# One accumulator per PSUM bank, attention output scaled into SBUF, layer-1 weight bounds by TensorE products, and a new planned order

## The chip, the core and the metric

The kernel runs on one core of a Trainium2 chip. The core has TensorE (matrix products, which stand in the profile as PE, with its weight loads apart as PEld), VectorE (DVE), ScalarE (ACT), GpSimd (POOL) and the SyncE queue (SP), which issues all DMAs here. The metric is the device time of one execution in microseconds (us), lower is better. Every instruction stands in its engine's queue in program order; an instruction that waits holds up all that stand behind it on that engine.

## The reference

Attention over 4 batches, 8 heads, 576 positions and head size 64, with a bias from a small network, then two pairs of dense layers on the 2304 x 512 result:

```python
scores = scale * q @ k.T
x = log1p(|i - j|) / log1p(max(i, 1))            # i, j: positions
scores = scores + relu(x * w1 + b1) @ w2          # one bias per head
attn = exp(scores - max(scores)); attn = attn / (sum(attn) + 1e-9)
x = (attn @ v) as [2304, 512]
x = (s * relu(x @ w_in)**2 + b) @ w_out           # layer 1: 512 -> 2048 -> 512
h = x @ w_in2; return (h - tanh(h)) @ w_out2      # layer 2: 512 -> 2048 -> 512
```

The four big weight matrices arrive as 64-bit floats, all else as 32-bit floats.

## The kernel before

**Arithmetic.** Each operand of a product is split into two 16-bit floats, a high and a low part, under a power-of-two scale, and each product is taken as three (high x high, high x low, low x high). The scales need bounds: the largest norm of the weights of layer 1 is found on the chip before they are split.

**Stages.** (1) Start, to about 150 us: VectorE turns the 64-bit weights of layer 1 into 32-bit (three instructions a piece, L1248, L1251, L1254), they are bounded (squares on ScalarE, L1306 and L1347; column sums by TensorE against ones, L1313), scaled and split (L619 high, L622 low; the high part may go to ScalarE or VectorE). Meanwhile q, k, v are prepared, the bias network is worked out (L726 and L729 hidden units, L760 product) and the first attention units run. (2) Attention and layer 1 overlapped, to about 575 us: 160 units (one head and one chunk of 128 rows each, or two heads of 64 rows) in 36 groups of four, 9 blocks of 256 rows for layer 1. (3) The rest of layer 1 from about 575 to 707 us, while the weights of layer 2 are converted and split. (4) Layer 2 to the end: Strassen-like products of 24 matrix instructions each (L2019 in, L2149 out).

**A unit**: scores into PSUM (L1040, two units at a time), bias added and maximum taken (VectorE, L1072), exponential (ScalarE, L1086), high and low part (L1096 or L1098, and L1103 on GpSimd or VectorE), a DMA transpose, then 14 matrix instructions into the accumulator `xp` (L1131, L1137). After the four units of a group: the row sums are inverted, `xp` is multiplied by them in place (VectorE, L1184), copied to a 16-bit high part (L1192 or L1194), the low part is the difference (L1198), and ScalarE squares `xp` for the norm (L1201). All four read the accumulator in PSUM.

**Layer 1, a block**: 16 products of 12 matrix instructions into `ph` (L1554), two at a time, relu (L1567), square (L1572), split (L1578/L1580, L1584); then 4 accumulators `po`, each of 4 products of 12 (L1626, 48 instructions in all), each moved out by L1645 (ScalarE) or L1640 (VectorE) in two or three pieces.

**PSUM** has 8 banks: 4 for scores (ring `s`), 2 for `ph` and small sums (ring `h`), one for `po`, one for `xp`. The tile `po` is [128, 2, 256] and `xp` too: two halves of one bank are used in turn, and the planner's rings `o` and `x` have two places each.

**Order.** A planner (`Schedule`) writes the whole program. Every task has its engines with a cost (`COST`, `XFER`), a due time with a correction from a table (`SHIFT`), a choice of engine (`ENGINE`), and rings that it takes places in; the planner walks through time with these figures, takes on each engine the task that is due first among those ready, and writes instructions in that sequence. When the program is built, waits are put in from what each instruction reads and writes; those of PSUM go by the whole bank, so an instruction on one half waits for one on the other half that stands ahead of it.

## Time and profile before

| | |
|---|---|
| runs, median (lowest to highest) | 1066.86 us (1065.9 to 1069.4) |
| the profiled execution | 1063.98 us, of it the span from first to last instruction 1062.2 us |
| busy in the span | PE 957.4 (90%), DVE 869.7 (82%), ACT 687.5 (65%), POOL 249.5 (23%) |
| mean granted clock of TensorE | 0.955 of full speed |

Busy shares are means over stages with different limits: in the start VectorE and ScalarE are full and TensorE is not, in the second half TensorE is. So the rows below are taken by stage. A busy PE need not be at its peak, since matrix instructions overlap.

### The profile page before, as it was taken

Reading aid. Unit: us, or ns where it says so; the run is one execution under the profiler, and the core shown is the slowest. Engines: PE = TensorE matmul, PEld = TensorE weight load, DVE = VectorE, ACT = ScalarE, POOL = GpSimd, SP = SyncE. Lnnn points to the kernel's source line nnn. Section 1 sums busy time; section 2 is a strip of 40 time slices with the busy share of each in tenths; the row PEclk is TensorE's granted clock in tenths of the full one; section 3 lists DMA queues with packets and bytes.
Section 4 is the critical chain, followed back from the end, with each engine's and each line's share of the span. In section 5 each row is a group of like instructions: output and inputs, shape, how many; then the busy total and the mean of one; then the engine's idle time right before and its main releaser. Section 6 shows DMA issues by size and latency. Waiting matters only on the chain.

```text
span 1062.2 us, 32293 instructions
## 1 busy us (share of the span) xinstructions
PE 957.4 (90%) x13370; PEld 821.9 (77%) x13370; DVE 869.7 (82%) x1902; ACT 687.5 (65%) x1357; POOL 249.5 (23%) x305
## 2 busy tenths in 40 slices
PE   5646679998999899999999998978999999999998
PEld 3213346787777788778877887868999999999998
DVE  6999997754658687878774879889999999898876
ACT  5998898668667586665734686866635546564433
POOL 6234455445456323355420000000000000000000
PEclk9867679999999999999999999999999999999999
DMA  9979998799999889989995905310111100100000
GB/s 344 395 233 247 308 211 171 165 241 234 221 186 232 167 188 190 186 157 198 166 172 94 399 13 162 117 40 2 32 32 42 42 22 25 39 22 23 23 22 22
DMA packets 261444, 153.66 MB, mean 145 GB/s; under 512 B 197680, under 2 KB 229552, under 8 KB 261296
## 3 DMA queue, kind: packets, MB, share of 16 engines
q1 hardware_dynamic: 261296, 151.59, 58.6%
q8 instruction: 104, 1.70, 0.7%
q14 instruction: 44, 0.36, 0.1%
HBM read 84.03 MB, written 20.33 MB: 98 GB/s over the span
## 4 chain that ended last, share of the span: by engine, by line
PE 70%; DVE 10%; ACT 9%; DMA 6%; issue 4%; SPq 1%; POOL 0%; DVEq 0%; ACTq 0%; POOLq 0%
PE po L1626 16%; PE ph L1554 14%; PE acc L2149 13%; PE pa L2019 8%; PE pb L2019 6%; PE sp L1040 4%; PE xp L1131 3%; PE po L2149 2%; DMA et<-hl 2%; PE pb L760 2%; ACT e L1086 2%; DVE sp L1072 1%; PE xp L1137 1%; ACT x L1645 1%; DMA w1big<-in_win 1%
## 5 line engine op out<-in xcount | busy, mean ns | idle before, releaser
L1626 PE MATMUL po<-hr,w1big 128*128 128x256 f16 x1728 | 203.3, 274 | 14.6 <-ACT x L1645 10.6
L1103 POOL TENSOR_TENSOR hl<-e,hl 128x512 f16<-128x512 f32 (+1 forms) x185 | 158.8, 871 | 191.5 <-ACT hl L1098 76.9
L1626 PEld LDWEIGHTS <-w1big 128*128 128x128 f16 x1728 | 166.4, 98 | 38.8 <-issue 19.4
L1554 PEld LDWEIGHTS <-w1big 128*128 128x128 f16 x1728 | 166.4, 99 | 31.0 <-issue 11.2
L2019 PEld LDWEIGHTS <-w2big 128*128 128x128 f16 x3024 | 175.1, 99 | 8.6 <-issue 8.6
L2149 PEld LDWEIGHTS <-w1big 128*128 128x128 f16 x3024 | 172.7, 98 | 0.0
L1086 ACT ACTIVATE e<-sp,mx 128x576 f32<-128x576 f32 x144 | 105.7, 736 | 57.8 <-POOL mx L1080 26.7
L1072 DVE CUSTOM_DVE_ANT_0 sp<-sp,bi 128x576 f32<-128x576 f32 x144 | 107.0, 775 | 34.9 <-PE sp L1040 30.1
L1554 PE MATMUL ph<-xt_own,w1big 128*128 128x256 f16 x960 | 115.1, 276 | 3.8 <-ACT r L1567 3.3
L1040 PE MATMUL sp<-ks,qs 64*128 64x288 f16 (+1 forms) x960 | 81.4, 299 | 19.5 <-ACT e L1086 19.2
L1554 PE MATMUL ph<-w1big 128*128 128x256 f16 x768 | 90.8, 276 | 0.3 <-DVE na L1513 0.3
L1131 PEld LDWEIGHTS <-et 128*128 128x128 f16 (+1 forms) x1440 | 55.8, 104 | 38.8 <-issue 21.4
L1040 PEld LDWEIGHTS <-qs 64*128 64x128 f16 (+1 forms) x960 | 46.0, 100 | 46.7 <-issue 33.6
L1131 PE MATMUL xp<-vp,et 128*128 128x64 f16 (+1 forms) x1440 | 65.7, 199 | 15.9 <-DMA et<-hl 6.3
L2149 PE MATMUL acc<-hr,w1big 128*128 128x128 f16 x1296 | 79.7, 219 | 0.0
L2149 PE MATMUL acc<-w2big,w1big 128*128 128x128 f16 x1296 | 79.2, 219 | 0.0
L1103 DVE TENSOR_TENSOR hl<-e,hl 128x512 f16<-128x512 f32 (+1 forms) x103 | 52.8, 526 | 12.3 <-ACT hl L1098 7.0
L2019 PE MATMUL pa<-w1big,w2big 128*128 128x128 f16 x960 | 61.2, 221 | 1.2 <-ACT w1big L2038 0.9
L1096 DVE CAST hl<-e 128x576 f16<-128x576 f32 x71 | 38.5, 543 | 24.5 <-ACT e L1086 17.4
L1645 ACT ACTIVATE x<-po,bcol,esc 128x128 f32<-128x128 f32 (+1 forms) x69 | 26.7, 443 | 48.6 <-PE po L1626 46.3
L1567 ACT ACTIVATE r<-ph 128x512 f32<-128x512 f32 x72 | 42.5, 592 | 19.3 <-PE ph L1554 18.1
L1098 ACT ACTIVATE hl<-e 128x576 f16<-128x576 f32 x73 | 48.9, 679 | 7.3 <-DMA et<-hl 6.9
(225 smaller groups left out, 1767.0 us busy)
## 6 DMA issues: line engine op xcount, KB each, us to landing
bi<-btd SPq DMA_DIRECT2D x64, 288.0 KB, 3.9
w1big<-in_wout SPq DMA_DIRECT2D x12, 1024.0 KB, 5.9
btd<-et SPq DMA_DIRECT2D x36, 295.5 KB, 4.5
w1big<-in_win SPq DMA_DIRECT2D x8, 1024.0 KB, 10.7
w2big<-in_win SPq DMA_DIRECT2D x8, 1024.0 KB, 13.0
x2d<-x SPq DMA_DIRECT2D x36, 128.0 KB, 2.0
w1big<-x2d SPq DMA_DIRECT2D x36, 128.0 KB, 2.3
outT<-xt_own SPq DMA_DIRECT2D x18, 256.0 KB, 2.2
```

The source lines that it names most:

```text
L1040: nc.tensor.matmul(out=out, lhsT=qs.tile[64 * h:64 * h + 64, sq, p * r:p * r + r], rhs=ks.tile[64 * h:64 * h + 64, sk, half * HS:(half + 1 ...
L1072: nc.vector.tensor_tensor_reduce(out=st, in0=st, in1=bi.tile.rearrange("p (a b) -> p a b", a=2), scale=-1.0 / KAP, scalar=3.0e38, op0=ALU. ...
L1086: nc.scalar.activation(out=put(e, row_tile("e")).rearrange("p (a b) -> p a b", a=2), in_=sp.tile[:, :, 0:HS], func=AF.Exp, scale=-1.0, bia ...
L1096: nc.vector.tensor_copy(out=h[:, 0:S], in_=e.tile)
L1098: nc.scalar.activation(out=h[:, 0:S], in_=e.tile, func=AF.Copy)
L1103: eng_of(eng).tensor_tensor(out=hl.tile[:, o:o + m], in0=e.tile[:, c:c + m], in1=hl.tile[:, c:c + m], op=ALU.subtract)
L1131: nc.tensor.matmul(out=xp[r0:r0 + r, o:o + 64], lhsT=et.tile[:, n, r0:r0 + r], rhs=vp.tile[:, 0, n % 5, 64 * h:64 * h + 64], start=n == 0, ...
L1554: nc.tensor.matmul(out=ph.tile[:, fi, :], lhsT=win_ap(1, sw, m, f), rhs=xa(sx, m), start=m == 0 and j == 0, stop=m == KM - 1 and j == 2,)
L1567: nc.scalar.activation(out=r.tile, in_=ph.tile, func=AF.Relu)
L1626: nc.tensor.matmul(out=po.tile[:, :NB1], lhsT=wout_ap(1, sw, f, c), rhs=rhl[f // 8][:, f % 8, sr, :], start=f == 0 and j == 0, stop=f == K ...
L2019: nc.tensor.matmul(out=bank.tile[:, f * HT:(f + 1) * HT], lhsT=w[:, sw, m, f * 128:(f + 1) * 128], rhs=xs[:, sx, m], start=p in (1, 2, 5) ...
L2149: nc.tensor.matmul(out=bank.tile[:, o + c * HT:o + (c + 1) * HT], lhsT=w[:, sw, f, c * 128:(c + 1) * 128], rhs=g[:, sx, f], start=new and ...
```

## The change

`po` and `xp` become one accumulator each: `po_tile` gives always the first half, `xp` shrinks to [128, 256], and the rings `o` and `x` have one place. The scaled attention output goes to a new SBUF tile `xf` (two buffers), and the high part, the low part and the squares read `xf`; the low part may now run on GpSimd. The bound of the layer-1 weights comes from TensorE: each 128-column block of a converted weight piece, read as its upper 16 bits, is multiplied by itself (16 matrix instructions for each of 8 weight parts), and VectorE takes maxima; the 16 squares on ScalarE and the 16 products against ones go. For the in-weights the maximum over partitions is taken with one more product against a unit matrix. The high part of a layer-1 weight may run on GpSimd. The tables and hop times of the planner are new, and with them the whole order. All lines below L455 shift, so `po` products are L1645, `ph` products L1573, `xp` products L1132 and L1138 in the new program.

```diff
@@ -28,13 +28,13 @@
-AHEAD = 8.71
+AHEAD = 6.97
 COST = {
...
@@ -42,16 +42,16 @@
-    0.98, "f.lo@dve": 0.98, "f.hi@act": 1.09, "f.hi@pool": 1.09, "u.hi@pool": 1.12, "u.ex@dve": 0.96,
...
@@ -59,152 +59,153 @@
-    "s1.lambda": "dve", "bias0.out": "act", "f0.hi": "act", "f1.hi": "act", "u7.hi": "act", "bias3.out": "act",
+    "s1.lambda": "dve", "f1.hi": "act", "bias3.out": "act", "bias4.lambda": "dve", "k1.hi": "act", "f2.hi":
...
-    ".begin": 3275.8, ".fn": -302.4, ".lambda": 973.3, "I0.add": -26.1, "I0.fn": 420.3, "I0.lambda": 110.4,
+    ".begin": 158.6, ".eye": 204.2, ".fn": -49.3, ".lambda": 60.6, "I0.add": 1197.4, "I0.fn": -551.5,
...
@@ -264,7 +265,7 @@
-    HOP = dict(pe=0.33, act=-0.03, dve=0.16, pool=0.4, turn=0.0)
+    HOP = dict(pe=0.57, act=-0.03, dve=0.16, pool=0.37, turn=0.0)
@@ -454,11 +455,9 @@
 
 
     po_all = ps_o.tile([128, 2, 256], F32, name="po")
-    po_n = [0]
 
     def po_tile():
-        po_n[0] += 1
-        return po_all[:, po_n[0] % 2, :]
+        return po_all[:, 0, :]
 
     ctx.enter_context(tc.manual_schedule())
 
@@ -569,12 +568,7 @@
-    xp_all = ps_x.tile([128, 2, 256], F32, name="xp")
-    xp_c = [0]
-
-    def xp_n():
-        xp_c[0] += 1
-        return xp_c[0] % 2
+    xp_all = ps_x.tile([128, 256], F32, name="xp")
@@ -586,8 +580,8 @@
-        ("bi", 4), ("e", 2), ("hl", 3), ("et", 4), ("stg", 4), ("qst", 1), ("qs", 2), ("ks", 8), ("vp", 8), ("s", 2), ("x", 2),
-        ("h", 2), ("o", 2), ("r", 2), ("xt", 4), ("x2", 2), ("xh", 2), ("sum", 4),
+        ("bi", 4), ("e", 2), ("hl", 3), ("et", 4), ("stg", 4), ("qst", 1), ("qs", 2), ("ks", 8), ("vp", 8), ("s", 2), ("x", 1),
+        ("h", 2), ("o", 1), ("r", 2), ("xt", 4), ("x2", 2), ("xh", 2), ("xf", 2), ("sum", 4),
@@ -615,6 +609,8 @@
     def copy_scale(out, in_, c, eng):
         if eng == DVE:
             nc.vector.tensor_scalar(out=out, in0=in_, scalar1=c, scalar2=None, op0=ALU.mult)
+        elif eng == POOL:
+            nc.gpsimd.tensor_scalar(out=out, in0=in_, scalar1=c, scalar2=None, op0=ALU.mult)
         else:
             nc.scalar.activation(out=out, in_=in_, func=AF.Copy, scale=c)
 
@@ -679,11 +675,16 @@
-        nc.vector.memset(ones16, 1.0)
+
+    def eye(_):
+        nc.gpsimd.affine_select(
+            out=eye32, in_=ones32, pattern=[[-1, 128]], compare_op=ALU.is_equal, fill=0.0, base=0, channel_multiplier=1,
+        )
+    t_eye = sc.add({POOL: 1.7}, eye, [t_one], prio=-1e5)
@@ -1122,7 +1123,7 @@
-                put(xp_i, xp_all[:, xp_n(), :])
+                put(xp_i, xp_all)
@@ -1179,28 +1180,32 @@
             nc.vector.reciprocal(out=sum_of[n].tile, in_=sum_of[n].tile)
         te = sc.add({DVE: 0.17}, recip, [te], d - 2, [], [sum_of[n]])
 
+        xf = inst("xf")
+
         def scale(_):
             x = xp_of[n].tile.rearrange("p (h d) -> p h d", d=64)
+            put(xf, x_p.tile([128, 256], F32, tag="xf", name="xf", bufs=2))
             nc.vector.tensor_tensor(
-                out=x, in0=x, in1=sum_of[n].tile.unsqueeze(2).to_broadcast([128, NP, 64]), op=ALU.mult,
+                out=xf.tile.rearrange("p (h d) -> p h d", d=64), in0=x,
+                in1=sum_of[n].tile.unsqueeze(2).to_broadcast([128, NP, 64]), op=ALU.mult,
             )
-        t_xs[n] = sc.add({DVE: 0.41}, scale, [t_pv[u] for u in us] + [te], d - 500, [], [sum_of[n], xp_of[n]])
+        t_xs[n] = sc.add({DVE: 0.41}, scale, [t_pv[u] for u in us] + [te], d - 500, [xf], [sum_of[n], xp_of[n]], share=0.0)
 
         def hi(eng):
             put(xh, x_p.tile([128, 512], F16, tag="xh", name="xh", bufs=2))
             if eng == DVE:
-                nc.vector.tensor_copy(out=xh.tile[:, 0:256], in_=xp_of[n].tile)
+                nc.vector.tensor_copy(out=xh.tile[:, 0:256], in_=xf.tile)
             else:
-                nc.scalar.activation(out=xh.tile[:, 0:256], in_=xp_of[n].tile, func=AF.Copy)
-        th = sc.add({DVE: 0.36, ACT: 0.45}, hi, [t_xs[n]], d - 100, [xh], [xp_of[n]], share=0.0)
-
-        def lo(_):
-            nc.vector.tensor_tensor(out=xh.tile[:, 256:512], in0=xp_of[n].tile, in1=xh.tile[:, 0:256], op=ALU.subtract)
-        th = sc.add({DVE: 0.42}, lo, [th], d - 100, [], [xh, xp_of[n]], share=0.0)
+                nc.scalar.activation(out=xh.tile[:, 0:256], in_=xf.tile, func=AF.Copy)
+        th = sc.add({DVE: 0.29, ACT: 0.45}, hi, [t_xs[n]], d - 100, [xh], [xf])
+
+        def lo(eng):
+            eng_of(eng).tensor_tensor(out=xh.tile[:, 256:512], in0=xf.tile, in1=xh.tile[:, 0:256], op=ALU.subtract)
+        th = sc.add({DVE: 0.43, POOL: 0.72}, lo, [th], d - 100, [], [xh, xf])
         t_xsq[n] = sc.add(
             {ACT: 0.42}, lambda _: nc.scalar.activation(
-                out=xp_of[n].tile, in_=xp_of[n].tile, func=AF.Square, accum_out=nrm[:, n:n + 1]
-            ), [th], d - 100, [], [xp_of[n]],
+                out=xf.tile, in_=xf.tile, func=AF.Square, accum_out=nrm[:, n:n + 1]
@@ -1281,7 +1286,7 @@
-                {ACT: 1.04, DVE: 0.72},
+                {ACT: 1.04, DVE: 0.72, POOL: 3.0},
@@ -1294,38 +1299,52 @@
+            if first:
+                put(pc, ps_h.tile([128, 512], F32, tag="h", name="pc"))
+            for d in range(4):
+                for j in range(2):
+                    w = w32_ap(i, j).bitcast(BF16).rearrange("p (n t) -> p n t", t=2)
+                    for m in range(2):
+                        x = w[:, m * 512 + d * 128:m * 512 + (d + 1) * 128, 1]
+                        nc.tensor.matmul(
+                            out=pc.tile[:, d * 128:(d + 1) * 128], lhsT=x, rhs=x, start=first and d + j + m == 0,
+                            stop=last and d == 3 and j == 1 and m == 1,
+                        )
+        return mm
+
     def norm_in_tasks(i, prio):
 
         pc = inst("h")
-        t, t_wsq[i] = None, []
-        for j in range(2):
-            sq = inst("r")
-
-            def square(_, j=j, sq=sq):
-                put(sq, r_p.tile([128, 2, NB1], F32, tag="r", name="sq").rearrange("p a n -> p (a n)").bitcast(BF16))
-                nc.scalar.activation(out=sq.tile, in_=w32_ap(i, j), func=AF.Square)
-            t_wsq[i].append(sc.add({ACT: 0.98}, square, [t_conv[i, j]], prio, [sq]))
-
-            def mm(_, j=j, sq=sq):
-                if j == 0:
-                    put(pc, ps_h.tile([128, 512], F32, tag="h", name="pc"))
-                for m in range(2):
-                    nc.tensor.matmul(
-                        out=pc.tile, lhsT=ones16, rhs=sq.tile[:, m * 512:(m + 1) * 512], start=j == 0 and m == 0,
-                        stop=j == 1 and m == 1,
-                    )
-            t = sc.add(
-                {PE: 0.45}, mm, [t_wsq[i][j], t_one, t], prio - 500, [pc] if j == 0 else [], [sq, pc]
-            )
+        t = sc.add(
+            {PE: 1.3}, gram_mm(pc, i, True, True), [t_conv[i, 0], t_conv[i, 1]], prio - 500, [pc]
+        )
+        t_wsq[i] = [t]
         return sc.add(
             {DVE: 0.66}, lambda _: nc.vector.tensor_reduce(out=wn[:, i:i + 1], in_=pc.tile, op=ALU.max, axis=AX.X),
             [t], prio, [], [pc],
             share=0.0,
         )
 
-    def scale_in(g):
+    def norm_max(g, deps, prio):
+
+        m = const.tile([128, 1], F32, name=f"wr{g}")
+
+        def wmx(_):
+            nc.vector.tensor_reduce(out=m, in_=wn[:, 2 * g:2 * g + 2], op=ALU.max, axis=AX.X)
+        t = sc.add({DVE: 0.17}, wmx, deps, prio, share=0.0)
+        pm = inst("h")
+
+        def mm(_):
+            put(pm, ps_h.tile([128, 512], F32, tag="h", name="pm")[:, :128])
+            nc.tensor.matmul(out=pm.tile, lhsT=m.to_broadcast([128, 128]), rhs=eye32, start=True, stop=True)
+        t = sc.add({PE: 0.5}, mm, [t, t_eye], prio - 500, [pm])
+        return sc.add({DVE: 1.2}, lambda _: scale_in(g, pm.tile), [t], prio - 400, [], [pm])
+
+    def scale_in(g, pm):
         m = const.tile([128, 1], F32, name=f"wm{g}")
-        nc.vector.tensor_reduce(out=m, in_=wn[:, 2 * g:2 * g + 2], op=ALU.max, axis=AX.X)
+        nc.vector.tensor_reduce(out=m, in_=pm, op=ALU.max, axis=AX.X)
         nc.vector.tensor_scalar(out=m, in0=m, scalar1=1.0625, scalar2=None, op0=ALU.mult)
         wn_g.append(m)
         cw[g] = pow2_scale(m, 1, f"w1_{g}")
@@ -1338,18 +1357,9 @@
...
-    def norm_out(i, j):
-        r = inst("r")
-
-        def square(_):
-            o = put(r, r_p.tile([128, 2, NB1], F32, tag="r", name="r")).rearrange("p a n -> p (a n)").bitcast(BF16)
-            k = (i - 4) * 2 + j
-            nc.scalar.activation(out=o, in_=w32_ap(i, j), func=AF.Square, accum_out=ssw[:, k:k + 1])
-        return square, r
-
-        nc.vector.tensor_reduce(out=s2, in_=ssw, op=ALU.add, axis=AX.X)
+        nc.vector.tensor_reduce(out=s2, in_=ssw[:, 0:2], op=ALU.max, axis=AX.X)
@@ -1421,7 +1431,7 @@
-        sc.add({DVE: 1.2}, lambda _, g=g: scale_in(g), [tr_in[2 * g], tr_in[2 * g + 1]], tin[4 * g + 4] + 1)
+        norm_max(g, [tr_in[2 * g], tr_in[2 * g + 1]], tin[4 * g + 4] + 1)
@@ -1448,8 +1458,17 @@
-            f, r = norm_out(i, j)
-            t_nout.append(sc.add({ACT: 1.08}, f, [t_conv[i, j]], tout[2 * (i - 4) + j] + 2, [r]))
+        a = i % 2 == 0
+        if a:
+            pg, t = inst("h"), None
+        d = tout[2 * (i - 4) + 1] + 2
+        t = t_wsq[i] = sc.add(
+            {PE: 1.3}, gram_mm(pg, i, a, not a), [t_conv[i, 0], t_conv[i, 1], t], d - 500, [pg] if a else [], [pg],
+        )
+        if not a:
+            def gmax(_, pg=pg, k=i // 2 - 2):
+                nc.vector.tensor_reduce(out=ssw[:, k:k + 1], in_=pg.tile, op=ALU.max, axis=AX.X)
+            t_nout.append(sc.add({DVE: 0.66}, gmax, [t], d, [], [pg], share=0.0))
...
@@ -2152,7 +2169,7 @@
-            {PE: 1.345}, mm, t_gl[k, p] + t_wp[1, s, p] + last_pe, base, [bank] + more if new else [], [bank] + more,
+            {PE: 1.345}, mm, t_gl[k, p] + t_wp[1, s, p] + last_pe, base, [bank] if new else [], [bank],
```

Three places in the order are shown, where the prediction rests on them. A word in brackets is the engine that the instruction waits for; `Activation` is ScalarE.

TensorE, layer 1 after the attention (stage 3), at a change from one `po` accumulator to the next. Before:

```order
L1626 MATMUL po<-hr,w1big 128x256
L1626 LDWEIGHTS w1big
L1626 MATMUL po<-hr,w1big 128x256 [waits Activation_49]
L1626 LDWEIGHTS w1big
L1626 MATMUL po<-hr,w1big 128x256
```

Now (the twelve `ph` pairs are cut to their first and last):

```order
L1645 MATMUL po<-hr,w1big 128x256
L1573 LDWEIGHTS w1big
L1573 MATMUL ph<-xt_own,w1big 128x256
...
L1573 MATMUL ph<-xt_own,w1big 128x256
L1645 LDWEIGHTS w1big
L1645 MATMUL po<-hr,w1big 128x256 [waits Activation_49]
```

Before, the first product of the next accumulator stands right behind the last of the old one and waits for ScalarE; now twelve products of another accumulator stand between. Of the 35 changes of `po` accumulator in the program 15 had nothing between before (6 in stage 2, 9 in stage 3); now 2 have nothing and one has two one-column sums, all three in the last block.

TensorE, stage 2, the first product of a group's attention output. Before:

```order
L1040 MATMUL sp<-ks,qs 128x288
L1131 LDWEIGHTS et [waits DMAHW5_49]
L1131 MATMUL xp<-vp,et 128x64 [waits Activation_49]
L1131 LDWEIGHTS et
L1131 MATMUL xp<-vp,et 128x64
```

Now:

```order
L1138 MATMUL xp<-vp,et 128x64
L1132 LDWEIGHTS et [waits DMAHW2_49]
L1132 MATMUL xp<-vp,et 128x64 [waits DVE_49]
L1132 LDWEIGHTS et
L1132 MATMUL xp<-vp,et 128x64
```

The wait for the accumulator was one for ScalarE (the squares, last of the four readers) and is now one for VectorE (the scaling, the only reader). Before, 33 of the group starts carry a wait for ScalarE; now 33 carry one for VectorE.

ScalarE, from the end of layer 1 into layer 2: `x` are evacuations of `po`, the rows with `w_1_c` splits of layer-2 output weights, and the row of 1280 columns the high part of the second part of the first layer-2 input. Before:

```order
L1645 ACTIVATE x_11520<-po,bcol,esc 128x64 x2
L619 ACTIVATE w1big<-w2big,w_1_c 128x1024 x3
L619 ACTIVATE w1big<-w1big,cols_139 128x1280
L619 ACTIVATE w1big<-w2big,w_1_c 128x1024 x2
L2038 ACTIVATE w2big<-pa,cols_139 128x512
```

Now:

```order
L615 ACTIVATE w1big<-w1big,cols_141 128x1280
L1664 ACTIVATE x_11595<-po,bcol,esc 128x128
L1664 ACTIVATE x_11595<-po,bcol,esc 128x64 x2
L615 ACTIVATE w1big<-w2big,w_1_c 128x1024 x2
L1664 ACTIVATE x_11683<-po,bcol,esc 128x128
L1664 ACTIVATE x_11683<-po,bcol,esc 128x64 x2
L615 ACTIVATE w1big<-w2big,w_1_c 128x1024 x3
L2057 ACTIVATE w2big<-pa,cols_141 128x512
```

The row of 1280 columns moved from behind the last evacuation and three weight splits to a place ahead of the last two evacuations.

## Rows read from the trace of the kernel before

**Rows 1.** Windows: stretch, length, busy us of PE, PEld, DVE, ACT, POOL; clock, DMA, GB/s

```profile
25.00:50.00 25.00, 14.56 (x120) 5.86 (x117) 24.62 (x52) 23.59 (x44) 6.96 (x3) 0.83 1.04 396
...
300.00:350.00 50.00, 47.56 (x663) 38.89 (x661) 34.00 (x75) 36.12 (x77) 28.83 (x32) 1.00 1.10 213
...
700.00:750.00 50.00, 40.48 (x614) 38.90 (x613) 46.53 (x77) 32.95 (x48) 0.00 (x0) 0.93 0.09 28
...
750.00:800.00 50.00, 50.00 (x897) 50.00 (x895) 49.25 (x110) 22.85 (x35) 0.00 (x0) 1.00 0.08 24
```

**Rows 2.** Timeline, 645 to 648: start, length, instruction, in brackets the idle time before

```profile
646.23 0.81 ACT L1645 ACTIVATE x<-po,bcol,esc 128x128 f32<-128x128 f32 x2 [1.27 <-PE po L1626]
...
647.09 1.14 PE L1626 MATMUL po<-hr,w1big 128*128 128x256 f16 x9 [0.90 <-ACT x L1645]
```

**Rows 3.** Waits of TensorE, 150 to 600: total, times, longest

```profile
PE po L1626 <- DVE x L1640: 4.0, 3, 2.9
...
PE xp L1131 <- DMA et<-hl: 3.4, 5, 1.3
...
PE po L1626 <- ACT x L1645: 2.5, 5, 0.9
...
PE xp L1131 <- ACT xh L1194: 2.1, 2, 1.6
...
PE xp L1131 <- ACT xp L1201: 1.5, 3, 0.9
...
PE xp L1131 <- DVE xh L1198: 1.4, 2, 0.8
```

**Rows 4.** Waits of TensorE, 590 to 730

```profile
PE po L1626 <- ACT x L1645: 8.1, 9, 1.2
...
PE pb L2019 <- ACT w1big L619: 2.9, 1, 2.9
...
PE pb L2019 <- DVE w1big L622: 1.9, 1, 1.9
```

**Rows 5.** Timeline, 711 to 715: the second part of the first input block

```profile
711.16 1.36 ACT L619 ACTIVATE w1big<-w1big,cols 128x1280 f16<-128x1280 f32 x1
...
712.57 0.22 PE L2019 MATMUL pb<-w1big,w2big 128*128 128x128 f16 x1 [2.87 <-ACT w1big L619]
...
713.09 1.55 DVE L622 SCALAR_TENSOR_TENSOR w1big<-w1big,cols 128x1280 f16<-128x1280 f32 x1
...
714.69 1.55 PE L2019 MATMUL pb<-w1big,w2big 128*128 128x128 f16 x13 [1.91 <-DVE w1big L622]
```

**Rows 6.** ScalarE lines: shapes, count, busy, mean ns, idle before

```profile
L1306 ACT ACTIVATE sq<-w1big 128x1024 bf16<-128x1024 f32 x8 | 8.5, 1058 | 4.1 <-DVE w1big L1254 4.1
...
L1347 ACT ACTIVATE r<-w1big 128x1024 bf16<-128x1024 f32 x8 | 8.4, 1052 | 0.1
```

**Rows 7.** VectorE lines

```profile
L1184 DVE TENSOR_TENSOR xp<-xp,sum 128x256 f32<-128x256 f32 x36 | 15.6, 433 | 16.7 <-PE xp L1137 16.5
...
L1072 DVE CUSTOM_DVE_ANT_0 sp<-sp,bi 128x576 f32<-128x576 f32 x144 | 107.0, 775 | 34.9 <-PE sp L1040 30.1 <-DMA bi<-btd 3.6 <-issue 0.2
...
L622 DVE SCALAR_TENSOR_TENSOR w1big<-w1big,w1o_c 128x1024 f16<-128x1024 f32 x8 | 12.0, 1534 | 0.1
...
L622 DVE SCALAR_TENSOR_TENSOR w1big<-w1big,w_c 128x1024 f16<-128x1024 f32 x8 | 10.1, 1273 | 0.0
...
L729 DVE TENSOR_SCALAR hid<-u_sb,cst_sb 128x528 f32<-128x528 f32 x4 | 1.9, 486 | 0.0
...
L1321 DVE TENSOR_REDUCE wn<-pc 128x1 f32<-128x512 f32 x4 | 2.7, 685 | 0.0
```

**Rows 8.** GpSimd lines

```profile
L1103 POOL TENSOR_TENSOR hl<-e,hl 128x512 f16<-128x512 f32 x88 | 109.4, 1245 | 112.5 <-ACT hl L1098 44.1 <-DVE hl L1096 42.4 <-issue 11.5
...
L729 POOL TENSOR_SCALAR hr<-u_sb,cst_sb 128x512 f32<-128x512 f32 x2 | 5.1, 2570 | 0.7 <-PE pb L760 0.7
```

**Rows 9.** TensorE lines

```profile
L867 PE MATMUL gram<-w1big 128*128 128x128 bf16 (+1 forms) x112 | 9.1, 235 | 9.1 <-DMA w1big<-in_kT 7.9 <-DMA w1big<-in_qT 1.0
```

More of the change, by code (lines that the diff above doesn't have):

```diff
@@ L664, in last_unit @@
         return max(units_of(**kw))
-    ones16 = const.tile([128, 128], BF16, name="ones16")
     onesh = const.tile([128, 1], F16, name="onesh")
     ones32 = const.tile([128, 128], F32, name="ones32")
+    eye32 = const.tile([128, 128], F32, name="eye32")
     cst_sb = const.tile([128, cst.shape[1]], F32, name="cst_sb")
@@ L1295, in w1_split, with gram_mm @@
         ]
+    def gram_mm(pc, i, first, last):
+        def mm(_):
[11 more added lines that the diff above has]
+        return mm
     def norm_in_tasks(i, prio):
         pc = inst("h")
[L1300 to L1319 removed]
+        t = sc.add(
+            {PE: 1.3}, gram_mm(pc, i, True, True), [t_conv[i, 0], t_conv[i, 1]], prio - 500, [pc]
+        )
+        t_wsq[i] = [t]
         return sc.add(
@@ L2131, in out_product @@
             st[j // 2] = inst("o" if j == 6 else "q")
-            st["more"] = [inst("o")] if j == 6 else []
         bank = st[j // 2]
         new = s == 0 and j % 2 == 0
-        more = st["more"] if j == 6 else []
         def mm(_):
@@ L2171, in psum_add @@
                     out=out(), in0=half(bank.tile, h), scalar=osc, in1=add(), op0=ALU.mult, op1=ALU.add
-                ), [t] + deps, pr, takes, list(uses) + [bank] + more, share=0.0,
+                ), [t] + deps, pr, takes, list(uses) + [bank], share=0.0,
             )
```

43 lines of the change are left out of this document (22 added, 21 removed), and 265 rows, old and new, of tables (ENGINE, SHIFT).

## The prediction

> **What bounds the kernel now.** I read the windows first, because the mean busy shares mix stages. In the start (25 to 50 us) VectorE works 24.62 of 25 us and ScalarE 23.59, TensorE 14.56: the reader is to see that TensorE waits there for weights and scores to be prepared. In the attention (300 to 350) TensorE works 47.56 of 50, VectorE 34.00, and the DMA engines stand at 1.10, as full as this view shows them. Around the turn to layer 2 (700 to 750) TensorE falls to 40.48 while VectorE works 46.53. In layer 2 (750 to 800) TensorE is full at 50.00 and VectorE nearly so at 49.25 [rows 1]. So work taken from TensorE's idle gaps counts after the start, work taken from VectorE counts in the start and near the turn, and work taken from ScalarE alone counts almost nowhere.
>
> Next I read the timeline at one change of accumulator, to learn what such a change costs. ScalarE starts to move the old `po` out at 646.23, and the first product of the new one follows at 647.09 after 0.90 us of idle time [rows 2]. The two accumulators are different halves of the bank, yet the new one waits for the evacuation of the old. So two places in one bank work as one here, and giving up the second half loses nothing. The waits of TensorE then give the sums: in the attention 4.0 + 2.5 us on `po`, 2.1 + 1.5 + 1.4 = 5.0 us on `xp` behind its four readers, and 3.4 us on the DMA transposes [rows 3]; after it 8.1 us on `po` in nine waits, 0.9 each [rows 4].
>
> **The change part by part.** All sums are made against the profiled execution's own 1063.98 us, 2.9 us under the median of the runs; I add 2.9 at the end. A difference of 0.3% (3.2 us) is what a measurement of this kernel can tell from none.
>
> *The accumulator `po`.* In the order, 15 of 35 changes had nothing between two accumulators, now two have nothing and one nearly nothing. Six of the 15 stood in the attention, where the waits cost 6.5 us [rows 3]. Filling them is worth between 0 (the filling work is then missing elsewhere) and 6.5; I take 5, since TensorE has other work ready there. Of the nine later ones six go for good: 6 x 0.9 = 5.4 [rows 4]. The ends are 0, if the twelve `ph` products put between are late themselves, and 8.1; I take 5.4, as their inputs were made long before in this stretch.
>
> *The accumulator `xp`.* Its readers fall from four to one, the scaling of 0.433 us [rows 7]. The high part, low part and squares then follow on SBUF. The 5.0 us of waits for them [rows 3] can go wholly, but a wait for the scaling stays on 33 group starts, and VectorE may take it late behind a 0.775 us score sum [rows 7]. Half, 2.5 us, is my value, ends 0 and 5.0.
>
> *The bound of the weights.* The sixteen squares go, 8.5 + 8.4 = 16.9 us of ScalarE [rows 6]. That engine is near full in the start, but it is VectorE that the chain to the first layer-1 product goes through: conversion, maximum, scale, low part. So by itself this is worth nothing, and it pays only through the work that can pass from VectorE to ScalarE. TensorE gets 128 products of 128 x 128; the same form took 9.1 / 112 = 0.081 us each in the preparation of q and k [rows 9], so 10.4 us. They lie in the start beside 10 us of idle time in every 25 [rows 1], so I cost them at nothing; without that cover they cost 10.4. VectorE gets two more maxima of 0.685.
>
> *VectorE in the start.* Ahead of the first block's layer-1 norm it loses twelve bias-network rows at 0.486 (-5.8), which go to ScalarE, and gets two more units' score sums (2 x 0.775 = 1.6), the two maxima (1.4) and four more small copies, counted at the 0.486 of a similar row (1.9) [rows 7]. The sum is -0.9.
>
> *Weight parts on GpSimd.* Five high parts of 128 x 1024 now run there: two of in-weights ahead of the first norm and three of out-weights later. The trace has none. The nearest rows are a 128 x 512 subtraction at 1.245 and a 128 x 512 scaling at 2.570 [rows 8]; twice these give 2.5 to 5.1 us a part on GpSimd, which has room (6.96 of 25). What a part costs VectorE is the question: nothing, or, if VectorE could not run beside it, the whole 5.1. The same VectorE split took 1.273 us with one set of weights and 1.534 with the other [rows 7]. The instruction is the same, so something beside it stretched it by 0.26 us; I put that down to GpSimd, though the row doesn't name it, and take one such stretch for each of five parts, 1.3 us. With the -0.9 the start comes to +0.4, which I call 0. Its ends are -0.9 (parts that cost VectorE nothing) and +24.8 (5 x 5.1 - 0.9).
>
> The row shows a slowdown of a fifth, not a standstill. The Trainium skill (SBUF — State Buffer, "SBUF: two separate sides") says that VectorE and GpSimd share a port pair that is locked for a whole instruction and that the loser blocks fully, if VectorE's instruction reads two SBUF operands or runs in a two-port mode. By that rule a part could cost VectorE its whole length; by the row it costs 0.26. I go by the row, but the rule is the slower rival below, and it speaks against this change.
>
> *The turn to layer 2.* TensorE waited 2.87 us for the high part (1.36 on ScalarE) and 1.91 for the low part (1.55 on VectorE) of the 1280 columns [rows 5]. ScalarE now makes the high part before the last evacuations, so it is early; the low part waits for VectorE, which is full there (46.53 of 50). I take 1.5 off, ends 0 and 4.8.
>
> *What is late next.* The attention gets shorter by 7.5 us with as many transposes, and the DMA engines are full there. The wait for them can stay at 3.4 or grow; I let it double, which gives back 3.4.
>
> Sum: 0 - 5 - 2.5 - 5.4 - 1.5 + 3.4 = -11.0, a profiled 1053, and 1056 as a median.
>
> **The rivals.** *Transposes take the attention's gain.* With DMA at 1.10 the stretch cannot shrink, so 5 + 2.5 - 3.4 = 4.1 us of gain falls away: 1060. For it: the row of 300 to 350 and the existing waits. Against it: only 3.4 us of the 450 from 150 to 600 are waited for the transposes now.
>
> *VectorE sets the turn.* The weights of layer 2 must be converted and split by VectorE before layer 2 can run, and it is full from about 700 on. If TensorE arrives earlier, it waits longer, and 5.4 + 1.5 us are lost: -4.1, so 1063. For it: 46.53 and 49.25 of 50 [rows 1] and both waits of [rows 4] on weights' splits. Against it: ScalarE, with 32.95 of 50, can take some.
>
> *GpSimd blocks VectorE.* If each of the five parts holds VectorE for its whole 5.1 us in the start, where it has 0.4 us free in 25, the start grows by 24.8, everything behind it shifts, and the later gains of 11.0 remain: +13.8, so 1078 on the profile's base and 1081 as a median, slower than before. It turns slower than before beyond the 3.2 us once a part costs VectorE more than (11.0 + 0.9 + 3.2) / 5 = 3.0 us. Against it: the 0.26 us seen.
>
> *The stalls only move.* The wait for the bank may go elsewhere, if the filling work was what TensorE did anyhow; the places show it done, but total work of TensorE is unchanged, and its idle time may appear at another wait: 1067.
>
> **How the numbers follow.** The forecast has 0.50: 1056, its own range 1046 to 1062 by the ends of the `po`, `xp` and turn terms. The transposes' rival has 0.17 (1060), VectorE at the turn 0.15 (1063), the stalls that move 0.06 (1067), GpSimd blocking 0.12 (1081). Faster by over 0.3% (under 1063.7) takes the first, most of the second (0.15) and 0.09 of the third: 0.74. Within 0.3% are the rest of these (0.02 + 0.06) and the fourth: 0.14. Slower is the last, 0.12. The range 1043 to 1067 leaves out the last, half of the fourth and about 0.05 below, for the case in which the `po` and `xp` waits and both of the turn's go wholly.
>
> **What would show it.** Right: the waits of TensorE on `po` fall from 14.6 to under 5 us in all; those on `xp` halve and name the scaling; the first `ph` product of layer 1 comes within 2 us of its place before; TensorE works over 42 of the 50 us around the turn. GpSimd's rows for the weight parts give their price, and VectorE's rows beside them show whether 0.26 us or the whole length is lost. Wrong: waits of TensorE for transposes over 7 us; VectorE idle between weight parts, or its split rows at several microseconds; the first `ph` product later by 5 us or more; a wait on layer-2 weight splits at the turn as long as the 4.8 us before.

## The result and the profile after

The changed kernel takes 1056.64 us (median of 4 runs, 1052.58 to 1059.28) against 1067.22 us of the kernel before (4 runs): a ratio of 0.9896, 95% interval 0.9858 to 0.9933. That is 10.6 us less; the forecast was 1056. Six more runs beside the kernel before gave 0.991 (0.989 to 0.9931).

The windows of the kernel after, with the columns of [rows 1]:

```profile
25.00:50.00 25.00, 16.62 (x136) 6.47 (x133) 24.62 (x52) 18.30 (x33) 5.85 (x2) 0.77 1.04 396
300.00:350.00 50.00, 43.33 (x582) 34.77 (x577) 37.79 (x95) 34.68 (x74) 16.45 (x25) 0.97 1.06 218
700.00:750.00 50.00, 44.34 (x700) 43.48 (x699) 48.43 (x78) 34.30 (x49) 0.00 (x0) 0.93 0.09 25
750.00:800.00 50.00, 50.00 (x897) 50.00 (x894) 47.69 (x107) 25.02 (x39) 0.00 (x0) 1.00 0.10 29
```

In the start ScalarE fell from 23.59 to 18.30 us of 25, while VectorE stayed at 24.62: the start is no shorter. From 700 to 750 TensorE works 44.34 us instead of 40.48, and VectorE 48.43 instead of 46.53.

TensorE's waits of the kernel after, 150 to 600, against [rows 3]:

```profile
PE sp L1041 <- ACT e L1087: 8.8, 14, 2.3
PE xp L1132 <- DMA et<-hl: 5.6, 6, 2.5
PE ph L1573 <- ACT r L1586: 2.9, 3, 2.0
...
PE po L1645 <- DVE x L1659: 0.8, 2, 0.5
```

and 590 to 730, against [rows 4]:

```profile
PE psum L695 <- DVE w2big L2064: 3.9, 1, 3.9
PE po L1645 <- ACT x L1664: 2.7, 2, 1.6
PE ph L1573 <- ACT r L1586: 1.9, 3, 1.4
```

The longest wait for the relu falls before 590. From 571.7, the end of the attention, to 735 its row is this:

```profile
PE ph L1573 <- ACT r L1586: 4.0, 4, 2.0
```

The waits that were to go are gone or small: in the attention `po` fell from 6.5 to 0.8 us and the waits for the readers of `xp` from 5.0 to nothing; later `po` fell from 8.1 to 2.7, and the two waits of [rows 5] at the turn went. In their places stand others: score products for exponentials (0.8 before), after the attention `ph` products for the relu that frees their bank (4.0 us in four waits), and one wait of 3.9 us for VectorE at the turn.

What that is worth is read from the length of each stretch. I took four marks from the timelines: the start of the first `po` product, the end of the last product of the attention output, the end of the last `po` product, and the start of the 303rd of layer 2's 3024 input products. Each kernel has two profiled executions here:

| stretch (us) | before | before, 2nd | after | after, 2nd |
|---|---|---|---|---|
| start to first `po` product | 198.6 | 197.2 | 200.0 | 197.8 |
| to the end of the attention | 374.6 | 373.2 | 371.8 | 369.2 |
| to the end of layer 1 | 133.8 | 133.8 | 132.0 | 130.1 |
| to the 303rd product of layer 2 | 32.6 | 32.6 | 30.1 | 29.0 |
| to the last product | 318.5 | 318.5 | 318.3 | 318.3 |

By means: +1.0, -3.4, -2.7, -3.1 and -0.2, in all -8.4. The profiled executions of before (1063.98 and 1061.19) are shorter than its median, so the last two of the 10.6 us are not located. The start is not resolved either: four executions that have the changed kernel's start unaltered (both of these, `halves` and `adjacent` below) reach the first `po` product between 197.8 and 202.5 us.

### The profile page after: what moved, and what is told of

It is laid out like the page before. It is cut to its first block, busy times and chain, and to the rows that moved or that the text cites. A ratio compares the mean times of both kernels' runs of the same rounds, so it can differ in the third digit from the quotient of the medians.

```text
span 1056.2 us, 32450 instructions
## 1 busy us (share of the span) xinstructions
PE 964.1 (91%) x13486; PEld 833.2 (79%) x13486; DVE 881.6 (83%) x1918; ACT 667.5 (63%) x1307; POOL 250.1 (24%) x319
## 4 chain that ended last, share of the span: by engine, by line
PE 43%; DVE 9%; ACT 3%; DMA 2%; issue 2%; POOL 1%; SPq 0%; DVEq 0%; ACTq 0%; POOLq 0%
PE acc L2166 14%; PE pa L2038 9%; PE pb L2038 7%; PE po L1645 5%; PE ph L1573 4%; PE po L2166 2%; DMA et<-hl 2%; DVE w2big L1852 2%; DVE w2big L618 1%; PE sp L1041 1%; DVE w1big L618 1%; ACT e L1087 1%; POOL hl L1104 1%; PE xp L1132 1%; DVE hr L1603 1%
## 5 line engine op out<-in xcount | busy, mean ns | idle before, releaser
L1645 PE MATMUL po<-hr,w1big 128*128 128x256 f16 x1728 | 202.9, 274 | 3.6 <-ACT x L1664 2.7
L1104 POOL TENSOR_TENSOR hl<-e,hl 128x64 f16<-128x64 f32 (+1 forms) x200 | 160.2, 818 | 184.9 <-ACT hl L1099 107.2
L1573 PEld LDWEIGHTS <-w1big 128*128 128x128 f16 x1728 | 166.9, 99 | 31.5 <-issue 10.6
L1645 PEld LDWEIGHTS <-w1big 128*128 128x128 f16 x1728 | 165.5, 98 | 26.5 <-issue 7.1
L1573 PE MATMUL ph<-xt_own,w1big 128*128 128x256 f16 x960 | 113.1, 274 | 3.0 <-ACT r L1586 2.2
L1041 PE MATMUL sp<-ks,qs 64*128 64x288 f16 (+1 forms) x960 | 84.2, 296 | 25.8 <-ACT e L1087 24.8
L1573 PE MATMUL ph<-w1big 128*128 128x256 f16 x768 | 91.2, 276 | 3.3 <-ACT r L1586 2.6
L1041 PEld LDWEIGHTS <-qs 64*128 64x128 f16 (+1 forms) x960 | 48.7, 99 | 53.0 <-issue 42.2
L1132 PEld LDWEIGHTS <-et 128*128 128x128 f16 (+1 forms) x1440 | 54.7, 104 | 41.2 <-issue 21.5
L1132 PE MATMUL xp<-vp,et 128*128 128x64 f16 (+1 forms) x1440 | 65.4, 199 | 19.1 <-DMA et<-hl 11.7
L1099 ACT ACTIVATE hl<-e 128x576 f16<-128x576 f32 x96 | 64.7, 678 | 23.1 <-DMA et<-hl 20.2
L1104 DVE TENSOR_TENSOR hl<-e,hl 128x512 f16<-128x512 f32 (+1 forms) x88 | 48.8, 572 | 15.9 <-ACT hl L1099 13.0
L1591 ACT ACTIVATE r<-r,sq 128x512 f32<-128x512 f32 x72 | 51.2, 718 | 0.9
L2074 ACT ACTIVATE w1big<-w1big 128x512 f32<-128x512 f32 x34 | 21.3, 630 | 45.6 <-DVE w1big L2064 33.4
```

The lines of the kernel that those rows point to most:

```text
L1041: nc.tensor.matmul(out=out, lhsT=qs.tile[64 * h:64 * h + 64, sq, p * r:p * r + r], rhs=ks.tile[64 * h:64 * h + 64, sk, half * HS:(half + 1 ...
L1099: nc.scalar.activation(out=h[:, 0:S], in_=e.tile, func=AF.Copy)
L1104: eng_of(eng).tensor_tensor(out=hl.tile[:, o:o + m], in0=e.tile[:, c:c + m], in1=hl.tile[:, c:c + m], op=ALU.subtract)
L1132: nc.tensor.matmul(out=xp[r0:r0 + r, o:o + 64], lhsT=et.tile[:, n, r0:r0 + r], rhs=vp.tile[:, 0, n % 5, 64 * h:64 * h + 64], start=n == 0, ...
L1573: nc.tensor.matmul(out=ph.tile[:, fi, :], lhsT=win_ap(1, sw, m, f), rhs=xa(sx, m), start=m == 0 and j == 0, stop=m == KM - 1 and j == 2,)
L1591: nc.scalar.activation(out=r.tile, in_=r.tile, func=AF.Square, scale=sq[:, fp // 4:fp // 4 + 1])
```

## The experiments

**A second look at both kernels.** Unaltered copies, no edit.

> The changed kernel unaltered, for a second profile and a narrower ratio. In the first profiled execution (1057.96 us) the attention ended only 1.5 us sooner than before (last attention product at 571.7 against 573.2), though TensorE's waits for the two accumulators fell there by 10.7 us; waits of score products for exponentials rose from 0.8 to 8.8. Theory 1 (the order of this plan makes the new wait, so it comes in every execution): score products wait for exponentials 7 to 10 us again and the last attention product stands at 570 to 573; the median stays near 1056.6. Theory 2 (that execution was an unlucky one, transfers landed late): the wait is under 5 us in this profile and the attention ends 4 us or more sooner than before.

Measured: 1055.76 us, profiled 1050.33. Score products waited 9.6 us for exponentials, as Theory 1 had it, so the new wait belongs to the plan. But the attention ended at 567.1, as Theory 2 had it. Both were half right: the wait is fixed, and the execution's length varies beside it.

> The kernel before unaltered, for a second profile. Two profiled executions of the changed kernel differ by 7.6 us in span (1056.2 and 1048.6); after 150 us the first has 20.5 us at the half clock, the second 10.2. Theory 1 (an execution's length goes by how long the clock was halved, and each kernel's length at equal clock is fixed): span minus half of the time at half clock after 150 us comes within 2 us of 1062.2 - 10.2 = 1052. Theory 2 (transfers or other delays vary too): it is off by more than 2 us.

Measured: 1061.19 us, span 1059.4, of it after 150 us 10.2 at half clock; span less half of that is 1054.3, off by 2.3. So Theory 2, narrowly. By the same sum the kernel after comes to 1046.0 and 1043.5. At equal clock the gain is thus 6.0 to 10.8 us. The clock accounts for 5.1 of the 7.6 us between the two executions of the changed kernel; for the kernel before it would make 5.1, where the spans differ by 2.8.

**Two halves of a bank again, the order kept.**

```
-        return po_all[:, 0, :]
+        po_n[0] += 1
+        return po_all[:, po_n[0] % 2, :]
...
-                put(xp_i, xp_all)
+                put(xp_i, xp_all[:, xp_n(), :])
```

> Two halves of a bank in turn for po and xp again, everything else and the order as in the changed kernel. Theory 1 (waits go by the whole bank, the second half was worth nothing): the same time within 0.3%, the same waits of TensorE on po and xp. Theory 2 (the second half lets the next accumulator begin earlier on the chip): 2 to 6 us faster, with fewer waits on po.

Measured: 1054.41 us, ratio 0.9908 (0.9884 to 0.9933), the same as the changed kernel's 0.991. Its waits of TensorE from 590 to 730:

```profile
PE psum L703 <- DVE w2big L2072: 3.9, 1, 3.9
PE po L1653 <- ACT x L1672: 2.6, 2, 1.5
PE ph L1581 <- ACT r L1594: 1.9, 3, 1.4
```

They are those of the changed kernel within 0.1 us. In this order the second half is worth nothing: one accumulator per bank neither costs nor gains by itself.

**The bound's products twice.** The matrix instruction of the bound is written twice in a row.

> Each of the 128 new products for the bounds of the layer-1 weights is made twice (the sum in the bank doubles, so the bound on the weights' norm is too large and the scale smaller). 128 more products of 0.092 us (11.8 us for 128 in the changed kernel's profile). Theory 1 (they lie beside VectorE's work in the start, cost nothing): within 3 us of the changed kernel, first layer-1 product within 2 us. Theory 2 (TensorE or the wait for the bound is on the path): 6 to 12 us slower, first layer-1 product later by as much.

Measured: 1057.06 us, 0.9928 (0.9906 to 0.9949), 1.9 us above the changed kernel at overlapping intervals; the first `ph` product came at 154.5 against 153.5 and 152.8. The two groups of 128 stand in two lines of 20.7 and 20.6 us:

```profile
L1311 PE MATMUL pc<-w1big 128*128 128x128 bf16 x128 | 20.7, 255 | 2.0 <-ACT et L615 2.0
L1315 PE MATMUL pc<-w1big 128*128 128x128 bf16 x128 | 20.6, 255 | 0.0
```

The products of the two lines alternate and overlap, so the two times are not to be added. The busy time of all products into `pc` together (columns PE, clock, DMA, GB/s) is 21.20 us here, first row, and 11.75 in the changed kernel, second row:

```profile
0.00:155.00 155.00, 21.20 (x256) 0.77 0.95 289
0.00:155.00 155.00, 11.75 (x128) 0.76 0.95 289
```

These 9.4 us more on TensorE in the start moved the total by 1.9 us, which the intervals do not tell from none: the products are covered, as Theory 1 had it.

**GpSimd's weight parts on ScalarE.**

```
-lambda e, j=j: copy_scale(pr[:, 0, ...], w32_ap(i, j), c(), e), deps, prio,
+lambda e, j=j: copy_scale(pr[:, 0, ...], w32_ap(i, j), c(), ACT if e == POOL else e), deps, prio,
```

> The five high parts of layer-1 weights that run on GpSimd (3.1 us each in the profile) run on ScalarE at the same place of the program. Theory 1 (a GpSimd part stretches one or two VectorE instructions beside it by about 0.7 us, 3.5 us in all, and these lie on the path of the start): the first ph product of layer 1 comes 2 to 4 us sooner and the total is 1 to 4 us lower. Theory 2 (the stretch is off the path, or ScalarE's five more microseconds cost as much): within 2 us. Theory 3 (ScalarE is what is late in the start): 2 to 5 us slower.

Measured: 1056.72 us, 0.9923 (0.9904 to 0.9943), by the ratios 1.4 us above the changed kernel at overlapping intervals, first `ph` product at 153.8: Theory 2. The timeline of the changed kernel shows what VectorE does beside one such part:

```profile
153.17 2.86 POOL L613 TENSOR_SCALAR w1big<-w1big,w1o_c 128x1024 f16<-128x1024 f32 x1 [0.76 <-DVE w1o_ic L488]
153.38 1.46 DVE L611 TENSOR_SCALAR w1big<-w1big,w1o_c 128x1024 f16<-128x1024 f32 x1
...
154.84 0.73 DVE L1073 CUSTOM_DVE_ANT_0 sp<-sp,bi 128x576 f32<-128x576 f32 x1
...
155.50 1.27 DVE L618 SCALAR_TENSOR_TENSOR w1big<-w1big,w1o_c 128x1024 f16<-128x1024 f32 x1
```

The part took 2.86 us (the five 2.85 to 3.49). Beside it VectorE's high part took 1.46 us, where the same form took 0.75 at 85.90 and 159.46; the score sum (0.73) and the low part (1.27) behind it ran at their usual length. Beside other parts it is another instruction (a low part of 1.95 us beside the part at 86.02, a copy of 1.30 instead of 0.45 beside that at 159.35):

```profile
86.02 3.34 POOL L613 TENSOR_SCALAR w1big<-w1big,w_c 128x1024 f16<-128x1024 f32 x1 [5.67 <-ACT hid L727]
...
86.76 1.95 DVE L618 SCALAR_TENSOR_TENSOR w1big<-w1big,w_c 128x1024 f16<-128x1024 f32 x1
```

With the parts on ScalarE, in this run's own timeline, the same low part and the same high part of VectorE took 1.28 and 0.74 us:

```profile
87.44 1.28 DVE L618 SCALAR_TENSOR_TENSOR w1big<-w1big,w_c 128x1024 f16<-128x1024 f32 x1
...
153.73 0.74 DVE L611 TENSOR_SCALAR w1big<-w1big,w1o_c 128x1024 f16<-128x1024 f32 x1
```

So the stretch comes from the GpSimd parts: one instruction is stretched by some 0.7 us a part, and none is held for the part's whole length.

**The scaled output left in PSUM, the order kept.**

```
-            put(xf, x_p.tile([128, 256], F32, tag="xf", name="xf", bufs=2))
+            put(xf, xp_of[n].tile)
...
-            eng_of(eng).tensor_tensor(out=xh.tile[:, 256:512], in0=xf.tile, ...
+            nc.vector.tensor_tensor(out=xh.tile[:, 256:512], in0=xf.tile, ...
```

The edit also gives the bank its two halves again, and it moves the 17 low parts that ran on GpSimd to VectorE, so its price is that of both.

> The scaled attention output stays in its accumulator again (two halves in turn) and the high part, the low part and the squares read it there; the 17 low parts that ran on GpSimd run on VectorE, which can read PSUM. The planned order is that of the changed kernel, so group starts come as early as there. Theory 1 (the waits for the four readers were worth 2.5 to 5 us of TensorE): waits on xp for the high part, low part and squares come back, 3 us or more, and the total is 2 to 6 us higher than the changed kernel's 1056. Theory 2 (TensorE in the attention is held by something else, as score products by exponentials, and the waits only change their name): within 2 us of the changed kernel.

Measured: 1060.83 us, 0.9941 (0.9924 to 0.9957): by the ratios 3.3 us above the changed kernel, whose interval (0.989 to 0.9931) just overlaps. TensorE's waits from 150 to 600:

```profile
PE sp L1049 <- ACT e L1095: 6.5, 12, 2.1
PE xp L1140 <- DVE xh L1211: 4.3, 5, 2.1
...
PE xp L1140 <- ACT xh L1207: 2.4, 2, 2.0
PE xp L1140 <- ACT xp L1214: 2.0, 5, 0.5
...
PE xp L1140 <- DVE xh L1205: 1.4, 2, 0.9
```

The waits for the readers are back (4.3 + 2.4 + 2.0 + 1.4 = 10.1; L1205 is the high part made by VectorE), while those of score products fell from 8.8 or 9.6 to 6.5, and the waits for transposes (5.6 or 3.0) are not in its list. Theory 1: of some 10 us of waits 3.3 reach the total.

**Four changes of `po` without filler, the order otherwise kept.** After planning, five `ph` products are moved to stand before the last quarter of the old accumulator:

```
+            for n, t in enumerate(mid):
+                if self.ready_at(t, dst + n, where(t)):
+                    src = where(t)
+                    self.log.insert(dst + n, self.log.pop(src))
```

Here `mid` are the `ph` products between two accumulators, and `dst` is the place of the old accumulator's last quarter.

> The changed kernel with its planned order kept but for five ph products after the attention, each moved one place ahead, so that four changes of po which had twelve ph products between have nothing between again. Nothing else moves. Theory 1 (an adjacent change costs 0.9 us and the filler hides it): TensorE's waits on po after the attention rise by about 3.6 us from 2.7, and the total is 3 to 5 us higher than the changed kernel's. Theory 2 (the filler only brings the next wait, ph for the relu that frees its bank, 4.0 us in four waits in the changed kernel): po waits rise by 3.6 but ph waits fall by 2 to 4, and the total stays within 2 us.

Measured: 1060.86 us (11 runs), 0.994 (0.9917 to 0.9962), 3.2 us above the changed kernel by the ratios, with intervals that overlap a little. Waits of TensorE, 590 to 730:

```profile
PE po L1685 <- ACT x L1704: 7.2, 7, 1.6
PE psum L735 <- DVE w2big L2104: 3.9, 1, 3.9
...
PE ph L1613 <- ACT r L1626: 0.5, 2, 0.3
```

`po` rose by 4.5 us, five waits of 0.9 in the timeline, one more than the four I had counted, and `ph` fell by 1.4. The stretch from the end of the attention to the end of layer 1 took 136.0 us, against 130.1 to 132.0 in the six executions here that have the changed kernel's order in it. Theory 1 for the most part; a third of the wait does move.

**Filler put into the kernel before, the order otherwise kept.** The same kind of edit, four `ph` products moved to stand ahead of the first product of the next accumulator.

> The kernel before with its planned order kept but for four ph products after the attention, each moved ahead into a change of po that had nothing between. Theory 1: po waits after the attention fall from 8.1 to about 4.5 and the total is 3 to 5 us lower than before's. Theory 2: the ph products now wait for the relu of their bank, or TensorE reaches layer 2 earlier and waits there for weights; the total stays within 2 us.

Measured: 1069.91 us, 1.0036 (1.002 to 1.0053): slower, which neither theory had. `po` waited 8.5 us in nine waits, as before. The timeline shows why:

```profile
650.78 1.47 PE L1665 MATMUL po<-hr,w1big 128*128 128x256 f16 x12
652.29 0.81 ACT L1684 ACTIVATE x<-po,bcol,esc 128x128 f32<-128x128 f32 x2 [2.58 <-PE po L1665]
653.15 1.03 PE L1665 MATMUL po<-hr,w1big 128*128 128x256 f16 x8 [0.90 <-ACT x L1684]
```

The twelve products at 650.78 are already the first quarter of the new accumulator: ScalarE had sat idle for 2.58 us, and moved the old one out only after them. In that order the evacuation stands behind the first quarter, and the wait comes 12 products into the accumulator. It is the same in the kernel before, where the wait at 647.09 stands there too. The filler was a quarter too early and hid nothing. Of the loss about 2 us lie in this stretch, where a `ph` product now waits 1.6 us for its relu; some 4 lie in the attention, where its order is that of the kernel before, and stay unexplained.

**New orders.** Four programs that the planner orders anew. In the first, the changed kernel takes the halves for separate:

```
-        ("h", 2), ("o", 1), ("r", 2),
+        ("h", 2), ("o", 2), ("r", 2),
```

> The changed kernel with two halves of the po bank and two places in the planner's ring o, so that the planner takes the halves for separate again; tables as in the changed kernel. In its order 15 changes of po have nothing between (6 in the attention, 9 later), as in the kernel before, instead of 2. Theory 1 (0.9 us a change): TensorE's waits on po go from 3.5 to about 15 us, 5.4 us of them after the attention, and the total is 5 to 10 us higher than the changed kernel's 1056. Theory 2 (filling only moves the wait): waits on po rise, but the total stays within 3 us.

In the second, the kernel before takes them for one: `("x", 1)` and `("o", 1)`.

> The kernel before with one place each in the planner's rings o and x (it now knows that the halves exclude each other), and its own tables; nothing else of the change. In its order 4 changes of po have nothing between (1 in the attention, 3 in the last block) instead of 15. Theory 1 (the planned exclusion is the greater part of the gain): 4 to 9 us faster than the kernel before, most of it after the attention, where po waits fall from 8.1 to about 3. Theory 2 (the tables are fitted to one order, and a new order loses elsewhere what it gains): within 3 us of the kernel before or slower.

In the third and fourth, the tables (`AHEAD` to `SHIFT`, and `HOP`) change places between the two programs; the planner's default transfer cost and one factor in its code stay with their program.

> The changed kernel with the planner's tables and hop of the kernel before; the planner still knows that the halves exclude each other, and the order comes out new (3 changes of po with nothing between). After what two other new orders showed (12 to 22 us more at the turn to layer 2, because VectorE had not split its weights), Theory 1 (the tables are fitted to a program and the gain needs both): 10 us or more slower than the changed kernel, slower than before, most of it in the start and at the turn. Theory 2 (code and exclusion carry the gain, tables are polish): within 4 us of the changed kernel's 1056.

> The kernel before (arithmetic, two rings of two) with the tables and hop of the changed kernel; 15 changes of po with nothing between. Theory 1 (tables fitted to another program): 10 us or more slower than before, mostly at the turn, where VectorE is full and TensorE waits for weight splits. Theory 2 (the new tables are better in themselves): 2 us or more faster than before.

The five stretches are those of the table above, from one profiled execution each:

| | us | ratio to before | start | attention | layer 1's rest | turn | layer 2 |
|---|---|---|---|---|---|---|---|
| after | 1056.64 | 0.9896 | 200.0 | 371.8 | 132.0 | 30.1 | 318.3 |
| o2 | 1079.65 | 1.0112 (1.0095 to 1.0129) | 199.0 | 375.3 | 125.9 | 51.8 | 320.9 |
| rings1 | 1085.08 | 1.0164 (1.0147 to 1.0181) | 201.8 | 387.2 | 114.9 | 45.4 | 328.4 |
| old tables | 1086.69 | 1.0192 (1.016 to 1.0224) | 213.3 | 378.3 | 124.1 | 43.8 | 327.5 |
| new tables | 1083.8 | 1.016 (1.0134 to 1.0187) | 204.8 | 378.5 | 139.5 | 29.0 | 326.1 |

All four are slower than the kernel before. In `o2` the adjacent changes cost about what I had summed (`po` waits of 7.7 us after the attention instead of 2.7), but its loss is the turn. Its windows and its waits from 590 to 760:

```profile
700.00:710.00 10.00, 3.19 (x30) 2.86 (x28) 9.79 (x21) 7.07 (x9) 0.00 (x0) 0.73 0.04 13
710.00:720.00 10.00, 2.02 (x24) 1.90 (x22) 10.00 (x12) 3.51 (x4) 0.00 (x0) 0.67 0.04 13
720.00:730.00 10.00, 3.52 (x31) 3.19 (x31) 8.78 (x9) 5.32 (x5) 0.00 (x0) 0.50 0.14 40
```

```profile
PE pb L2046 <- ACT w1big L623: 10.9, 1, 10.9
PE po L1653 <- ACT x L1672: 6.7, 7, 1.1
PE pa L2046 <- ACT w1big L623: 4.9, 1, 4.9
```

The rest of layer 1 took 6 us less than in the changed kernel, and then TensorE worked 8.73 of 30 us while VectorE worked 28.57. The longest wait was for the high part of the second part of the first layer-2 input, the 1280 columns. ScalarE made it only at 721.46, when VectorE, busy with weights between, had finished the sums it is made from (L1927):

```profile
721.46 1.36 ACT L623 ACTIVATE w1big<-w1big,cols 128x1280 f16<-128x1280 f32 x1 [0.38 <-DVE w1big L1927]
...
722.88 0.27 PE L2046 MATMUL pb<-w1big,w2big 128*128 128x128 f16 x1 [10.85 <-ACT w1big L623]
```

So what TensorE waited for was the input of layer 2, late behind VectorE's work on the weights. `rings1` and the old tables lose 11 to 13 us against before at the turn too, with waits of `pb` for ScalarE's high parts of 6.1 and 9.0 us; they also lose 13 to 15 us in the attention or the start and 9 to 10 us in layer 2. So a planner that knows the bank's exclusion gains nothing by itself with the old tables (`rings1`: Theory 2), and the tables carry no gain to another program (Theory 1 twice, though the new tables lose in every stretch but the turn, where I had put the loss). Of these programs only the changed pair is faster than before.

## Why the prediction was right

The direction, the size and the main mechanisms were right. That the total was right within a microsecond is luck: after the attention the sum had twice what came, at the turn half, the start was taken as 0, and two of the 10.6 us are not located. The range of the forecast itself does not follow from its terms either: with the `po`, `xp` and turn terms at their upper ends, 0, the sum gives 1070, not 1062.

**The accumulator `po`.** The price of 0.9 us a change held (`adjacent`: 0.9 five times), and the waits after the attention fell by 5.4 us, as summed. But the stretch became only 1.8 to 3.7 us shorter: this term was too large, since `ph` products now wait for their relu, which I had taken for ready in this stretch. `adjacent`, which undoes this part for five changes, is 3.2 us slower.

In the attention the waits fell by 5.7, near my 5, but this agreement is luck. I had priced six changes with nothing between at the whole 6.5 us. In the timeline five of these six have no wait of 0.2 us or more, and the sixth has one of 0.34. The rest stands at changes that had other work between already; the longest is behind a score product:

```profile
355.73 0.29 PE L1040 MATMUL sp<-ks,qs 64*128 64x288 f16 x2
358.89 1.44 PE L1626 MATMUL po<-hr,w1big 128*128 128x256 f16 x6 [2.88 <-DVE x L1640]
```

These waits went with the new order; no run shows by which part of it.

One reading was off, in the section on the change too: by the trace the wait of [rows 2] stands 12 products into the new accumulator, not at its first one. The price is the same, the place is not, and `fill` failed on it.

**The accumulator `xp`.** Worth 3.3 us (`xf_undone`, with the move of 17 low parts in it) where I had 2.5. The wait for the scaling, for which I had kept half of the 5.0, came to 0.2 us in one execution of the changed kernel and to none in the other.

**What is late next.** I let the transposes take 3.4 us back. They waited 5.6 and 3.0 in the two executions, so no steady growth; what came instead is the score products' wait for exponentials, 8.8 and 9.6 us. What makes the exponentials late is open. The three attention terms gave -4.1, the stretch -3.4 by the means: right size, but the `po` term by luck, and another taker.

**The start.** Forecast 0; measured +1.0 by the means to the first `po` product, and +2.0 to the first `ph` product (153.5 and 152.8 against 151.2 and 151.1), the limit that I had set. VectorE's sum was incomplete: I had counted four more small copies, and up to the first `ph` product it made six more of the bias outputs alone (ten in 4.8 us instead of four in 1.9). The products of the bound are covered (`gram_twice`), and GpSimd's parts cost 0.7 us of VectorE each instead of 0.26, off the path (`whi_act`). What makes up the microsecond is open, and no run puts the squares back on ScalarE. The slower rival, 5.1 us a part, is excluded. The Trainium skill (SBUF — State Buffer, "SBUF: two separate sides") has VectorE block fully behind a GpSimd instruction that holds the shared ports, if it reads two operands from SBUF or runs in a two-port mode. The trace agrees that something is held, for some 0.7 us a part, but not for the whole: the low part at 86.76, which reads two, took 1.95 us instead of 1.28 and ended at 88.71, inside the part that ran from 86.02 to 89.36 (GpSimd's times are rough).

**The turn.** Forecast -1.5; measured -3.1. Both waits of [rows 5] went, and one of 3.87 us for VectorE took their place. A third wait from 590 to 730, which I had not listed, went too:

```profile
PE pb L2019 <- ACT w2big L2038: 1.9, 1, 1.9
```

This account goes by the waits and the stretches; no run puts the high part of the 1280 columns back behind the evacuations. The rival on VectorE at the turn named the right engine: it holds the turn in this kernel and in `o2`, but here the gain was not eaten.

## What to carry to other kernels

A wait between two accumulators in one PSUM bank is priced by the idle time in the timeline, but look also at where in the accumulator it stands: the evacuation may be queued behind the first products of the next one, and then a filler at the change hides nothing. Price each wait at the place where it stands: a sum of waits by name puts those at one kind of change down to another (in the attention 0.34 of 6.5 us stood where I had looked). Of waits removed on a full engine a third to seven tenths came out as gain here (3.3 of 10.1 us for `xp`, 3.2 of 4.5 for `po`): the next input in line is late too, unless it was seen to be early. A tuned order belongs to its program: here each of four programs with one changed and the other not lost 12 to 20 us, three of them most or much of it at the turn, where VectorE was full.
